# First attention scores issued between the last projection products, and the first keys loaded from ScalarE's queue

## The chip, the cores and the metric

One core of one Trainium2 chip runs the whole kernel. The metric is the device time of one execution in microseconds (us); a smaller one is better. The time before is 1726.04 us, the median of 3 runs (1724.21 to 1727.97).

## The reference, cut to what matters

A transformer block on `x` of 2048 rows by 512, with 32 heads of width 16, all in float32:

```python
mod = (silu(c) @ w_mod).reshape(1, 6, 1, -1)        # sa, ca, ga, sb, cb, gb
h = layernorm(x) * (1 + ca) + sa
q, k, v = heads(h @ wqkv)                            # 3 x (32, 2048, 16)
p = softmax(q @ k.T * 16 ** -0.5)                    # (32, 2048, 2048)
x = x + ga * ((p @ v) @ wo)
h = layernorm(x) * (1 + cb) + sb
x = x + gb * (gelu(h @ w1 + b1) @ w2 + b2)
```

## The kernel before, in words

Each float32 operand of a projection is split into a high and a low part, and a product is three matmuls per 128 rows of contraction. The order of all work is written out by hand (`manual_schedule`): what a loop emits first on an engine runs first there. DMAs go out on SyncE's queue (SP), a few early ones on ScalarE's. All DMAs, of both queues, take eight semaphores in turn, and an issue waits until the DMA that used its semaphore before has landed; the next instruction of that queue waits behind it.

**Projections (up to about 265 us).** A loop over four blocks of 512 rows makes the first keys and queries (`proj_qk`, evacuated at L446 to L461, stored to DRAM at L464) and some values (`proj_v`, L486, stored at L488). `split_w` (L183, L184) makes weight parts, `mod_store` (L232) a small product. In the last block the kernel opens the tiles `kts` and issues, in this order on SP, the queries of unit 0 (`load_qm(0)`, six DMAs, L515), half of its keys (`build_k`, six DMAs, L504) and the queries of unit 1.

Then a loop over `items` (L773, L776) makes the remaining values, keys and queries, twelve matmul pairs an item, the second half of an item six places behind the first. Between them `half_slot` runs the first pass over the scores, which finds row maxima: a matmul L573 into a `mx` bank, for one half of the keys a Relu copy on ScalarE (L579), for the other a combined maximum on VectorE (L582). `evacuate` copies a finished item on ScalarE (L446), GpSimd splits it (L450, L451), SP stores it (L464).

A unit `u` is a group of four heads and a block of 512 queries; there are 32 units, the first four of group 0. `load_q(u)` brings a unit's queries into `qst` (six DMAs, L515) and then its maxima (two DMAs, L535). Before, `load_q(0)` is issued at item `nv + 19` and `load_q(1)` at `nv + 21`, both within the items loop.

**Attention (from about 265 us).** At its start SP issues the constant rows of a new key tile, twelve loads of 256 KB (keys of groups 1 and 3, L504), two rows `ga_b` and `gb_b`, and the values of group 1. The loop runs over steps `s`, sixteen for each unit, in an order of tokens:

```python
ORDER = ("X0 X1 M1 X2 M0 X3 P M1".split(), "X0 X1 X2 M0 M0 X3 P M1".split())
ORDER_END = "X0 X1 X2 X3 P".split()       # step 0 and the last unit
```

X0 to X3 are `exp_step`: a matmul L1010 of 128 keys (stationary) with the unit's 512 queries and an Exp on ScalarE (L1011) into a tile `p`. M is one matmul and reduce of the remaining maxima (L554, L556). P is `pv_step` of the step before: eight matmuls L843. After a unit's last P, L830 copies its output. Step 16 is the first that reads `qst` of unit 1. `load_q(u + 1)` stands in step `16 u + 2` for `u` of 1 and more.

PSUM has eight banks. In the items loop three are the ring `sc` and five the ring `mx`; for attention they are dealt out again (four `sc`, three `mx`, one `pv`).

Of the kernel before, what the change touches and what calls it, by code (L numbers as in the profile page):

```python
# [16 lines left out]
P = 128  # L17
# [20 lines left out]
NU1 = len(FRONT) - 1  # L38
LAG = 6
REST_AT = 3  # L40
OP0 = 1
OPN = 4
NWARM = 18
# [10 lines left out]
def block_kernel(ctx: ExitStack, tc: tile.TileContext, x, wqkv, wo, w1, b1, w2, b2, c, w_mod, out):  # L54
# [439 lines left out]
    def heads(src, g, part, a, t0, t1):  # L494
        r0 = (g % 2) * 64
        ap = src[part, r0 : r0 + 64, t0:t1]
        return ap.rearrange("(p a d) t -> a d p t", a=2, d=DH)[a]

    def build_k(dst, src, g, t0=0, t1=S, parts=(0, 1, 2)):
        for i in parts:  # L500
            part = (0, 0, 1)[i]
            for a in range(2):
                r0 = a * 64 + i * DH
                sy.dma_start(dst[r0 : r0 + DH, :, t0:t1].bitcast(F32), heads(src, g, part, a, t0, t1))  # L504

    def load_k(g, tile):
        kst[g] = tile
# [29 lines left out]
    def one_rows(k):  # L537
        for a in range(2):
            r0 = a * 64 + KR
            sy.dma_start(k[r0 : r0 + 2].bitcast(F32), one_d[:, None, :].to_broadcast([2, 2, S]))  # L540

    mxs, left, vpos = {}, {}, {}

# [91 lines left out]
    for b in range(NB):  # L635
        if b == NB - 1:
            close(lcm)
            kcm, kpool = pool("kpool")
            kts = [kpool.tile([P, 2, S], FR, name=f"kt{i}") for i in range(2)]
            qmcm, qmpool = pool("qmpool")  # L640
            kd[0], kd[1] = kts
            load_qm(0)
            build_k(kts[0], kd_d[0], 0, 0, 2 * TB)
            load_qm(1)
        if b:
            if b + 1 < NB:
                xn = ln1(b + 1)()
            if b + 2 < NB:
                load_x(b + 2)
        accs = first  # L650
        if b:

            accs = {w: bank() for w in (1, 0)}
            terms = {w: terms3(*qk_args(b, 0, w)) for w in (1, 0)}
            n1 = 2 * KC
            for i0, i1 in ((0, n1), (n1, len(terms[0]))):
                for w in (1, 0):
                    for i in range(i0, i1):
                        te.matmul(accs[w], *terms[w][i], start=i == 0, stop=i == len(terms[w]) - 1)
        proj(proj_qk, b, 0, 1, accs[1])  # L660
        if b == 1:
            load_w(1)
            st[0] = sy
        if b == NB - 1:
            rest()
            rest = lambda: None
            split_w(1)
        proj(proj_qk, b, 0, 0, accs[0])
        if b == 0:
            xn = ln1(1)()  # L670
        if b == NB - 1:
            mod_store(mrow)
            break
        if b == 1:
            mod_cols(1, mrow)
        for _ in range(V_A[b][0]):
            proj(proj_v, *vitems.pop(0), len(vitems) == 15)
        ln1_t(b + 1, xn)
        for _ in range(V_A[b][1]):
            proj(proj_v, *vitems.pop(0))  # L680
        if b < 2:
            mrow = mod_rows(wms)
        if b == 0:
            wms = [load_wm(2, 0), load_wm(5, 1)]
# [36 lines left out]
    for n in range(N + 2):  # L721
        if n == 1:
            close(acm)
        if n == 0:
            build_k(kts[0], kd_d[0], 0, 2 * TB, S)
        if n == 3:
            load_qm(FRONT[2])
        if n == 5:
            load_w(2)
        if n == 7:  # L730
            build_k(kts[1], kd_d[0], 1)
        if n == nv + 5:
# [12 lines left out]
        if n == nv + 10:  # L745
            kd[2] = kts[0]
            build_k(kts[0], kd_d[1], 2)
        if n == nv + 16:
            load_v(0)
        if n == nv + 19:  # L750
            load_k(2, kts[0])
        if n == nv + 19:
            load_q(0)
        if n == nv + 21:
            load_q(1)
        if n < N:
            k, b, w = items[n]
            if k and b == 2 and w and k < 3:
                split_w(k + 1)
            if n:  # L760
                acc[n] = bank()
                terms[n] = terms3(*qk_args(b, k, w)) if k else terms3(*v_args(b, w), late_b=False)
        new = []
        if n == 0:
            rest()
            rest = evacuate(0)
        for i in range(NT if n else 0):


            m, j = divmod(n * NT + i - NT - LAG, NT)  # L770
            if n < N:
                p, q = terms[n][i]
                te.matmul(acc[n], p[:64], q[:64], start=i == 0, stop=False)  # L773
            if 0 < m < N:
                p, q = terms[m][j]
                te.matmul(acc[m], p[64:], q[64:], start=False, stop=j == NT - 1)  # L776
            t = n * NT + i - NT
            for _ in range(len(slots) * (t + 1) // NS_B - len(slots) * t // NS_B):
                visit()
            if i == REST_AT:  # L780
                rest()
                rest = lambda: None
            if 0 < m < N and j == NT - 1:
                rest = evacuate(m)
                if m == N - 1:
                    break
        for q in (late, todo):
            if q:
                q.pop(0)()
        todo += new  # L790
    rest()
    close(wcm)
    close(hcm)
    close(tcm)

    sc, mx = rings["sc"], rings["mx"]
    set_rings(sc=(sc[0], sc[1], mx[0], sc[2]), mx=mx[1:4], pv=mx[4:])


    pcm, ppool = pool("ppool", bufs=2)  # L800
# [1 line left out]
    one_rows(kq[1])  # L802
    load_k(1, kts[1])
    load_k(3, kq[1])
    epool = ctx.enter_context(tc.tile_pool(name="epool", bufs=1, side="right"))

    wo_hi = epool.tile([P, KC, D], FR, name="wo_hi")
    wo_lo = epool.tile([P, KC, D], FR, name="wo_lo")
    x2a = [epool.tile([P, 4, D], F32, name=f"x2a{i}") for i in range(2)]
    b2_b, ga_b, gb_b = [epool.tile([P, D], F32, name=n) for n in ("b2_b", "ga_b", "gb_b")]  # L810
    for i, t in enumerate((ga_b, gb_b)):
        sy.dma_start(t, bass.AP(tensor=g_d.tensor, offset=g_d[i].offset, ap=[[0, P], [1, D]]))
    o_b = epool.tile([P, 4, D], F32, name="o_b")
    xn_b = epool.tile([P, 4, D], F32, name="xn_b")

    wo_r = {}

    def wo_load(k):
        wo_r[k] = epool.tile([P, D], F32, tag="h32", name="wo_raw", bufs=3)
        sy.dma_start(wo_r[k], wo[k * P : (k + 1) * P, :])  # L820
        if k == 0:
            sy.dma_start(b1_c, b1.rearrange("(f p) -> p f", p=P))
            sy.dma_start(b2_b, bass.AP(tensor=b2.tensor, offset=b2.offset, ap=[[0, P], [1, D]]))

    pt = {}

    def attn_out(u, pv):
        g, qb = divmod(u, NB)
# [23 lines left out]
    def at(s, f):  # L852
        hooks.setdefault(s, []).append(f)

    for k in range(KC):
        s0 = 20 + 8 * k
        at(s0, lambda k=k: wo_load(k))
        at(s0 + 3, lambda k=k: gp.tensor_tensor(wo_r[k], wo_r[k], ga_b, op=ALU.mult))
        at(s0 + 4, lambda k=k: ve.tensor_copy(wo_hi[:, k], wo_r[k]))
        at(s0 + 6, lambda k=k: gp.tensor_tensor(wo_lo[:, k], wo_r[k], wo_hi[:, k].bitcast(F32), op=ALU.subtract))  # L860
# [138 lines left out]
    for i, n in zip(range(4, 9), (12, 13, 13, 14, 14)):  # L999
        at(base + n, lambda i=i: run("l", lambda: ln2(0), i))  # L1000

    def exp_step(s, j):

        u, kc = divmod(s, NKC)
        q, k = qst[u], kst[u // NB]
        p, a = divmod(j, 2)
        ps = bank()
        pb = pt[s, j] = ppool.tile([P, TB], F32, tag="p", name="p", bufs=10)
        r0 = a * 64
        te.matmul(ps, k[r0 : r0 + KX, p, kc * P : (kc + 1) * P], q[r0 : r0 + KX, p], start=True, stop=True)  # L1010
        ac.activation(pb, ps, AF.Exp, scale=SCALE)  # L1011

    for s in range(NS):
        u, kc = divmod(s, NKC)
        g, qb = divmod(u, NB)
        if kc == 2 and 0 < u < NU - 1:
            load_q(u + 1)
        new = []
        for tok in ORDER[s % 2] if 0 < s < NS - NKC else ORDER_END:
            if tok[0] == "X":  # L1020
                exp_step(s, int(tok[1]))
            elif tok[0] == "P":
                if s:
# [12 lines left out]
    pv_step(NS - 1)  # L1036
    for cm in (pcm, qcm, vgcm, kqcm, qmcm):
        close(cm)


# [134 lines left out]
```

## Time and profile before

| what | value |
|---|---|
| median of 3 runs | 1726.04 us (1724.21 to 1727.97) |
| the profiled execution's own time | 1728.43 us |
| its span, from first to last instruction | 1726.7 us |
| mean granted TensorE clock | 0.993 |
| TensorE (PE) busy | 1715.8 us |
| VectorE (DVE) busy | 1389.9 us |
| ScalarE (ACT) busy | 1352.9 us |
| DMA queue q1, share of 16 engines | 32.6% |

PE is the matmul unit, PEld its weight loads, SPq the issuing of DMAs on SyncE's queue. A busy PE isn't PE at its peak: matmul ends are modelled, so the number of instructions in a stretch says more than its busy time. `PEclk` is the granted TensorE clock as a share of full speed. In the timeline a row has start, duration, engine, line, tiles and count; in brackets stands the idle time of the engine before it and what ended it.

### The profile page before, as it was taken

To read this page: it belongs to the slowest core of one execution; us is meant where nothing else is said; L and a number is where in the kernel's file an instruction comes from. 1 tells how busy PE (TensorE), PEld (TensorE's weight loads), DVE (VectorE), ACT (ScalarE), POOL (GpSimd) and SP (SyncE) were. 2 spreads that over 40 slices of the span, in tenths; PEclk is the share of its full clock that TensorE was granted. 3 is DMA by queue.
4 is the path that set the end of the run, shared out by engine and by line. 5 is a ranking of instruction groups with operands and counts; after the bars stand their busy time and mean duration, and the time that the engine had idled before them with its cause. 6 is when DMAs were issued, how large, how long until landed. Compare 5 with 4: busy or idle time off the path is not lost.

```text
span 1726.7 us, 29970 instructions
## 1 busy us (share of the span) xinstructions
PE 1715.8 (99%) x10968; PEld 905.6 (52%) x10968; DVE 1389.9 (80%) x2559; ACT 1352.9 (78%) x2580; POOL 312.7 (18%) x341
## 2 busy tenths in 40 slices
PE   9999999999999999999999999999999999999998
PEld 7766664333443334333433343334433488888887
DVE  6699997998888888888888888888885296746453
ACT  3588888999999999999999999999999632222222
POOL 3205430110000000000000000000022154636562
PEclk9899998999999999999999999999999999999999
DMA  9854988314112201400500110111023064423331
GB/s 328 223 124 153 172 177 162 73 41 60 40 36 44 55 24 33 69 23 24 88 23 23 43 33 24 39 32 27 23 66 106 19 204 131 138 79 110 99 122 49
DMA packets 125223, 144.22 MB, mean 84 GB/s; under 512 B 39026, under 2 KB 74866, under 8 KB 123124
## 3 DMA queue, kind: packets, MB, share of 16 engines
q1 hardware_dynamic: 123828, 139.71, 32.6%
q10 hardware_dynamic: 1248, 2.59, 0.4%
q8 instruction: 86, 1.41, 0.4%
q14 instruction: 61, 0.50, 0.1%
HBM read 106.37 MB, written 35.87 MB: 82 GB/s over the span
## 4 chain that ended last, share of the span: by engine, by line
PE 95%; DVE 2%; ACT 1%; SPq 1%; DMA 1%; issue 1%; POOL 0%; ACTq 0%
PE pv L843 30%; PE mx L554 20%; PE sc L1010 14%; PE sc L308 9%; PE mx L1074 6%; PE mx L573 5%; PE sc L776 4%; PE pv L1074 2%; PE sc L950 2%; PE sc L773 2%; PE mx L950 1%; PE sc L261 0%; PE sc L359 0%; DMA wmod<-in_w_mod_dram 0%; DVE bst L239 0%
## 5 line engine op out<-in xcount | busy, mean ns | idle before, releaser
L1011 ACT ACTIVATE p<-sc 128x512 f32<-128x512 f32 x2048 | 1054.7, 613 | 43.1 <-PE sc L1010 16.8
L556 DVE TENSOR_REDUCE mxs<-mx 128x1 f32<-128x512 f32 x1472 | 928.1, 683 | 118.8 <-PE sc L1010 91.4
L843 PE MATMUL pv<-p,vg 128*32 128x512 f32 x4096 | 548.1, 607 | 0.0
L1010 PE MATMUL sc<-qst,kq 50*128 50x512 f32 x1024 | 286.8, 438 | 0.3 <-ACT raw L446 0.3
L1010 PE MATMUL sc<-qst,kt 50*128 50x512 f32 x1024 | 282.5, 432 | 0.0
L554 PE MATMUL mx<-kq,qmx 48*128 48x512 f32 x768 | 262.5, 428 | 0.5 <-DVE mxs L556 0.4
L554 PEld LDWEIGHTS mx<-kq,qmx 48*128 48x128 f32 x768 | 121.9, 184 | 230.4 <-DVE mxs L556 212.1
L554 PE MATMUL mx<-kt,qmx 48*128 48x512 f32 x704 | 241.1, 430 | 0.0
L554 PEld LDWEIGHTS mx<-kt,qmx 48*128 48x128 f32 x704 | 113.6, 186 | 211.0 <-DVE mxs L556 191.5
L1053 ACT ACTIVATE g<-sc,b_c 128x512 f32<-128x512 f32 x56 | 38.6, 690 | 223.0 <-PE sc L308 218.5
L595 POOL CAST m<-mn 128x16 fp32r<-128x16 f32 x32 | 6.3, 198 | 1040.8 <-DVE mn L589 1040.8
L582 DVE CUSTOM_DVE_ANT_0 cp<-mx,cp 128x512 f32<-128x512 f32 x288 | 182.1, 686 | 14.0 <-PE mx L573 11.2
L573 PE MATMUL mx<-kt,qmx 48*128 48x512 f32 x576 | 181.1, 428 | 2.9 <-DMA qmx<-qk 1.2
L579 ACT ACTIVATE cp<-mx 128x512 f32<-128x512 f32 x288 | 157.2, 603 | 26.2 <-PE mx L573 20.9
L843 PEld LDWEIGHTS pv<-p,vg 128*32 128x32 f32 x4096 | 81.1, 108 | 181.3 <-issue 169.7
L1010 PEld LDWEIGHTS sc<-qst,kq 50*128 50x128 f32 x1024 | 126.8, 186 | 30.3 <-ACT p L1011 21.3
L573 PEld LDWEIGHTS mx<-kt,qmx 48*128 48x128 f32 x576 | 102.5, 190 | 57.7 <-DVE mxf L582 34.3
L1057 DVE TENSOR_TENSOR glo<-g,ghi 128x512 fp32r<-128x512 f32 x56 | 57.6, 1029 | 92.1 <-ACT ghi L1056 92.1
L1010 PEld LDWEIGHTS sc<-qst,kt 50*128 50x128 f32 x1024 | 125.6, 185 | 9.4 <-ACT p L1011 2.4
L879 POOL TENSOR_TENSOR w1l<-w1r,w1h 128x512 fp32r<-128x512 f32 x56 | 76.5, 1366 | 146.7 <-DVE w1h L878 123.1
L881 POOL TENSOR_TENSOR w2l<-w2r,w2h 128x512 fp32r<-128x512 f32 x56 | 82.5, 1473 | 6.2 <-DVE w2h L880 5.8
L308 PE MATMUL sc<-kt,w1h 128*128 128x512 f32 x224 | 73.8, 391 | 0.0
(185 smaller groups left out, 1912.5 us busy)
## 6 DMA issues: line engine op xcount, KB each, us to landing
qk<-parts SPq DMA_DIRECT2D x30, 512.0 KB
w1r<-in_B_w_dram SPq DMA_DIRECT2D x56, 256.0 KB
w2r<-in_B_w_dram SPq DMA_DIRECT2D x56, 256.0 KB
qmx<-qk SPq DMA_DIRECT2D x192, 64.0 KB
qst<-qk SPq DMA_DIRECT2D x192, 64.0 KB
kq<-qk SPq DMA_DIRECT2D x24, 256.0 KB
kt<-qk SPq DMA_DIRECT2D x24, 256.0 KB
vg<-v SPq DMA_DIRECT2D x8, 664.0 KB
```

Source lines behind the costliest of these rows:

```text
L308: te.matmul(ps, p, q, start=i == 0, stop=i == len(terms) - 1)
L554: te.matmul(ps, qmx[u][rows, p, qc * P : (qc + 1) * P], kst[u // NB][rows, p, kr * TB : (kr + 1) * TB], start=True, stop=True)
L556: ve.tensor_reduce(mxs[u][:, p, a, qc, kr : kr + 1], ps, axis=AX.X, op=ALU.max, negate=True)
L573: te.matmul(ps, qmx[u][rows, p, qc * P : (qc + 1) * P], kd[u // NB][rows, p, t0 : t0 + TB], start=True, stop=True)
L579: ac.activation(vpos[n, a], ps, AF.Relu)
L582: ve.tensor_tensor_reduce(v, ps, v, -1.0, 3.0e38, ALU.add, ALU.min, mxs[u][:, p, a, qc, r : r + 1])
L843: te.matmul(cur_pv[0][32 * j : 32 * (j + 1)], vg[g][:, kc, j * VW : j * VW + 32], pt.pop((s, j)), start=kc == 0, stop=kc == NKC - 1)
L879: gp.tensor_tensor(alo, a, ahi.bitcast(F32), op=ALU.subtract)
L881: gp.tensor_tensor(blo, b, bhi.bitcast(F32), op=ALU.subtract)
L1010: te.matmul(ps, k[r0 : r0 + KX, p, kc * P : (kc + 1) * P], q[r0 : r0 + KX, p], start=True, stop=True)
L1011: ac.activation(pb, ps, AF.Exp, scale=SCALE)
L1074: te.matmul(acc[qb][t], p[:, sl], q, start=f == 0 and n == 0, stop=f == NF - 1 and n == 2)
```

## The change

Three edits, and what they need.

1. `build_k` gets a queue as an argument. The six DMAs of unit 0's first keys go out on ScalarE's queue, and in program order they stand ahead of `load_qm(0)`, whose six DMAs stay on SP. In the order of instructions ScalarE's six stand behind the copy L486 and ahead of the copy L453 that evacuates the last block's first product; the fourth, fifth and sixth wait for semaphores that the first, third and fifth query DMA of unit 0 used.
2. The four `exp_step`s of step 0 run inside the items loop, between the last matmuls of the last item (places 9, 11, 13 and 15 of the tail that `FIRST_X` counts). They use two `sc` banks (the third holds the last item) and write to four tiles that exist already or are opened for them. Step 0 of the attention loop skips its X tokens. The pool `epool`, whose space overlaps two of these tiles, is opened after step 1.
3. `load_q(1)` moves from item `nv + 21` to step 2 of attention. On SP it then stands behind the constant rows, the twelve key loads, four stores of maxima, `ga_b`, `gb_b` and the values of group 1.

```diff
+FIRST_X = (9, 11, 13, 15)
...
-    def build_k(dst, src, g, t0=0, t1=S, parts=(0, 1, 2)):
-        for i in parts:
+    def build_k(dst, src, g, t0=0, t1=S, eng=sy):
+        for i in range(3):
...
-                sy.dma_start(dst[r0 : r0 + DH, :, t0:t1].bitcast(F32), heads(src, g, part, a, t0, t1))
+                eng.dma_start(dst[r0 : r0 + DH, :, t0:t1].bitcast(F32), heads(src, g, part, a, t0, t1))
...
+            build_k(kts[0], kd_d[0], 0, 0, 2 * TB, ac)
             load_qm(0)
-            build_k(kts[0], kd_d[0], 0, 0, 2 * TB)
             load_qm(1)
...
-        if n == nv + 21:
-            load_q(1)
+        if n == N:
...
+            first_p.extend([px, pm, wraw[:, 0], wraw[:, 1]])
...
+                if n == N - 1:
+                    last_sc = rings["sc"].pop()
...
+            if n >= N and (n - N) * NT + i in FIRST_X:
+                exp_step(0, FIRST_X.index((n - N) * NT + i))
...
-    set_rings(sc=(sc[0], sc[1], mx[0], sc[2]), mx=mx[1:4], pv=mx[4:])
+    set_rings(sc=(sc[0], mx[0], sc[1], last_sc), mx=mx[1:4], pv=mx[4:])
...
+    at(1, open_epool)
...
-        if kc == 2 and 0 < u < NU - 1:
+        if kc == 2 and u < NU - 1:
             load_q(u + 1)
...
             if tok[0] == "X":
-                exp_step(s, int(tok[1]))
+                if s:
+                    exp_step(s, int(tok[1]))
```

More of the change, by code (lines that the diff above doesn't have):

```diff
@@ L540, in one_rows, with exp_step @@
             sy.dma_start(k[r0 : r0 + 2].bitcast(F32), one_d[:, None, :].to_broadcast([2, 2, S]))
+    pt, first_p = {}, []
+    def exp_step(s, j):
+        u, kc = divmod(s, NKC)
+        q, k = qst[u], kst[u // NB]
+        p, a = divmod(j, 2)
+        ps = bank()
+        pb = pt[s, j] = ppool.tile([P, TB], F32, tag="p", name="p", bufs=10) if s else first_p[j]
+        r0 = a * 64
+        te.matmul(ps, k[r0 : r0 + KX, p, kc * P : (kc + 1) * P], q[r0 : r0 + KX, p], start=True, stop=True)
+        ac.activation(pb, ps, AF.Exp, scale=SCALE)
     mxs, left, vpos = {}, {}, {}
@@ L753, in block_kernel @@
             load_q(0)
-        if n == nv + 21:
-            load_q(1)
+        if n == N:
+            wraw = tpool.tile([P, 2, KC, P], F32, tag="wraw", name="p_w", bufs=1).rearrange("p a k n -> p a (k n)")
+            pm = tpool.tile([P, TB], F32, tag="pm", name="p_m", bufs=1)
+            pxcm, pxpool = pool("pxpool")
+            px = pxpool.tile([P, TB], F32, name="px")
+            first_p.extend([px, pm, wraw[:, 0], wraw[:, 1]])
         if n < N:
@@ L793, in block_kernel @@
     close(hcm)
-    close(tcm)
     sc, mx = rings["sc"], rings["mx"]
-    set_rings(sc=(sc[0], sc[1], mx[0], sc[2]), mx=mx[1:4], pv=mx[4:])
+    set_rings(sc=(sc[0], mx[0], sc[1], last_sc), mx=mx[1:4], pv=mx[4:])
     pcm, ppool = pool("ppool", bufs=2)
@@ L804, in block_kernel, with open_epool @@
     load_k(3, kq[1])
[L805 to L814, printed above, removed]
+    epool = wo_hi = wo_lo = x2a = b2_b = ga_b = gb_b = o_b = xn_b = None
+    def open_epool():
+        nonlocal epool, wo_hi, wo_lo, x2a, b2_b, ga_b, gb_b, o_b, xn_b
+        close(tcm)
+        epool = ctx.enter_context(tc.tile_pool(name="epool", bufs=1, side="right"))
+        wo_hi = epool.tile([P, KC, D], FR, name="wo_hi")
+        wo_lo = epool.tile([P, KC, D], FR, name="wo_lo")
+        x2a = [epool.tile([P, 4, D], F32, name=f"x2a{i}") for i in range(2)]
+        b2_b, ga_b, gb_b = [epool.tile([P, D], F32, name=n) for n in ("b2_b", "ga_b", "gb_b")]
+        for i, t in enumerate((ga_b, gb_b)):
+            sy.dma_start(t, bass.AP(tensor=g_d.tensor, offset=g_d[i].offset, ap=[[0, P], [1, D]]))
+        o_b = epool.tile([P, 4, D], F32, name="o_b")
+        xn_b = epool.tile([P, 4, D], F32, name="xn_b")
     wo_r = {}
@@ L823, in wo_load @@
             sy.dma_start(b2_b, bass.AP(tensor=b2.tensor, offset=b2.offset, ap=[[0, P], [1, D]]))
-    pt = {}
     def attn_out(u, pv):
@@ L1000, in block_kernel @@
         at(base + n, lambda i=i: run("l", lambda: ln2(0), i))
[L1002 to L1011, printed above, removed]
     for s in range(NS):
@@ L1036, in block_kernel @@
     pv_step(NS - 1)
-    for cm in (pcm, qcm, vgcm, kqcm, qmcm):
+    for cm in (pcm, pxcm, qcm, vgcm, kqcm, qmcm):
         close(cm)
```

## The prediction

> **What bounds the kernel now.** I read the page first, for the engine shares and the chain.
>
> ```profile
> PE 1715.8 (99%) x10968; PEld 905.6 (52%) x10968; DVE 1389.9 (80%) x2559; ACT 1352.9 (78%) x2580; POOL 312.7 (18%) x341
> PE 95%; DVE 2%; ACT 1%; SPq 1%; DMA 1%; issue 1%; POOL 0%; ACTq 0%
> ```
>
> TensorE is the chain. A microsecond in which it waits, or runs slowly, is lost unless another engine would have held it anyway. So I looked next, in tables by stretch, for time in which its clock fell. It did so in two places, both beside the change (columns: length, PE, PEld, DVE, ACT, POOL busy with counts, PEclk, DMA share, GB/s).
>
> ```profile
> 60.59:64.00 3.41, 3.41 (x17) 2.73 (x15) 0.00 (x0) 0.57 (x1) 0.93 (x1) 1.00 0.84 178
> 64.00:67.41 3.41, 3.41 (x14) 1.91 (x13) 1.98 (x3) 2.06 (x5) 0.79 (x1) 1.00 1.03 130
> 67.41:70.83 3.42, 2.26 (x10) 1.34 (x9) 0.69 (x1) 1.47 (x4) 1.73 (x2) 1.00 0.93 141
> 70.83:84.48 13.65, 13.65 (x52) 11.25 (x51) 7.85 (x23) 8.18 (x15) 0.00 (x0) 0.50 0.89 229
> 84.48:98.13 13.65, 13.44 (x104) 9.16 (x103) 12.83 (x41) 11.97 (x23) 0.00 (x0) 1.00 0.40 109
> 265.38:268.80 3.42, 3.12 (x16) 1.33 (x15) 2.31 (x10) 3.42 (x8) 1.73 (x4) 1.00 0.78 290
> 268.80:279.04 10.24, 10.24 (x45) 3.88 (x37) 5.27 (x9) 5.85 (x12) 0.52 (x1) 0.50 0.92 152
> 279.04:289.28 10.24, 10.24 (x75) 3.97 (x73) 8.84 (x15) 9.57 (x19) 0.00 (x0) 1.00 1.02 117
> ```
>
> After a thin stretch of matmuls (10 in 3.42 us, 16 in 3.42 us) the clock is at half, for 13.65 us and for 10.24 us. (The 14 and 17 ahead of 67.41 fill the 128 rows of the array; the 16 have 48 to 50 rows or 32 columns, as the rows below show of their kinds.) PE's busy time doesn't show it; the counts do. The first low clock costs between 13.65 x (1 - 23/41) = 6.0 us (by DVE's count) and 13.65 x (1 - 15/23) = 4.7 us (by ACT's); I take 5.3. For the second I count the P matmuls alone:
>
> ```profile
> 268.80:279.04 10.24, 4.82 (x24) 0.40 (x16) 0.50 0.92 152
> 279.04:289.28 10.24, 5.33 (x40) 0.79 (x40) 1.00 1.02 117
> ```
>
> 24 instead of 40: 10.24 x (1 - 24/40) = 4.1 us, or 0.4 us for each microsecond of low clock there.
>
> **Part 1, the tail of the projections.** Timeline of ScalarE and TensorE:
>
> ```profile
> 264.00 0.60 ACT L579 ACTIVATE cp<-mx 128x512 f32<-128x512 f32 x1 [0.33 <-PE mx L573]
> 265.24 0.60 ACT L446 ACTIVATE raw<-sc 128x512 f32<-128x512 f32 x1 [0.65 <-PE sc L776]
> 265.74 4.02 ACT L1011 ACTIVATE p<-sc 128x512 f32<-128x512 f32 x8
> ```
>
> Eight Exps in 4.02 us are 0.5 us each. Today all eight stand behind the last copy L446, and TensorE waits for them bank by bank. The change puts four (2.0 us) in front of that copy, where ScalarE has 0.33 + 0.65 = 1.0 us of idle time. So the copy comes 1.0 us later, and step 1's Exps start 1.0 us earlier. TensorE then has step 0's P at hand at once, and the thin stretch is filled. I expect the clock not to fall here: 1.0 + 4.1 = 5.1 us gained, if nothing later waits.
>
> **Part 2, `load_q(1)` behind the key loads.** This is what I weigh most. SP's queue, and TensorE at step 16:
>
> ```profile
> 253.49 3.83 SPq L515 DMA_DIRECT2D qst<-qk  x6
> ...
> 269.80 0.64 SPq L540 DMA_DIRECT2D kq<-one  x2
> 270.49 2.91 SPq L504 DMA_DIRECT2D kt<-qk  x6
> 275.22 11.32 SPq L504 DMA_DIRECT2D kq<-qk  x6
> ...
> 300.42 0.58 SPq L691 DMA_DIRECT2D vg<-v  x1
> 301.50 3.50 SPq L515 DMA_DIRECT2D qmx<-qk  x6
> ...
> 309.14 2.71 SPq L515 DMA_DIRECT2D qst<-qk  x6
> 311.89 1.28 SPq L535 DMA_DIRECT2D qst<-m  x2
> ```
> ```profile
> SPq L602 <- DMA kq<-qk: 7.0, 4, 1.8
> ```
> ```profile
> 303.57 0.72 PE L1010 MATMUL sc<-qst,kq 50*128 50x512 f32 x3
> ...
> 304.70 1.06 PE L843 MATMUL pv<-p,vg 128*32 128x512 f32 x8
> ```
> ```profile
> 306.06 0.63 ACT L830 ACTIVATE osb<-pv 128x512 f32<-128x512 f32 x1
> ```
>
> The P at 304.70 is unit 0's last, that of step 15: the copy of its output follows at 306.06. It stands within step 16, so the scores at 303.57 are step 16's, the first that need `load_q(1)`. Today that load is issued at 253.49, 50 us ahead. In the changed order it stands behind the twelve loads of 256 KB, directly behind the values `vg` and ahead of the `qmx` that was issued at 301.50. The DMA engines are full in that time (share 1.02 at 117 GB/s, the row from 279.04: 3.1 MB take 26 us), and the issues in between wait for these loads to land (the wait row). No row lets the queue go faster, and the change leaves the order ahead of it as it is.
>
> So `load_q(1)` is issued at about 301.5. Its eight DMAs take 4.0 us to issue (309.14 to 313.17 for unit 2), up to 305.5. How long the last takes to land no row tells directly: not below nothing, and not above the 4.0 us of a query DMA in the chain on a full queue (below). I take 2.5, as that queue is emptier by then. The last copy's 1.0 us delay reaches the stores that start this queue in part (GpSimd waits there for VectorE as well): 0.5. Step 16 can start at 305.5 + 2.5 + 0.5 = 308.5, from 306 to 310. Part 1 moves the wish for it to 303.57 - 5.1 = 298.5. TensorE issues in order, so the M and P tokens behind stand too, for 10 us, and ScalarE and VectorE run dry. Against before, step 16 starts 308.5 - 303.57 = **4.9 us later**. All that part 1 wins is eaten here, whether its clock stays up or not: the load sets the time.
>
> **Part 3, the clock after that wait.** Ten idle microseconds are far more than the thin stretches that brought the clock down twice. The same steps follow as from 268.80, so a low microsecond costs 0.4. If the low clock is counted from early in the wait, as long as 10.24 us, 2 us of it fall on work: 0.8. If it lasts 13.65 us of work: 5.5. I take the middle, **3.0 us**.
>
> The Trainium skill, page "TensorE: Matmul & The Clock Gate", section "Part 1: The HAM clock gate", says that the full clock returns after about 3.4 us of sustained work. By that the cost would be 3.4 x 0.4 = 1.4 us, an estimate from the page. This trace disagrees: under steady work the clock stayed low for 10.24 and 13.65 us.
>
> **Part 4, first keys on ScalarE's queue.** The start of the first pass:
>
> ```profile
> 56.88 4.29 SPq L515 DMA_DIRECT2D qmx<-qk  x6
> 61.21 3.98 SPq L504 DMA_DIRECT2D kt<-kd  x6
> 65.23 3.77 SPq L515 DMA_DIRECT2D qmx<-qk  x6
> ```
> ```profile
> 66.09 3.99 DMA qmx<-qk
> ```
> ```profile
> 59.21 0.60 ACT L486 ACTIVATE vst<-sc 128x512 f32<-128x512 f32 x1
> 63.43 0.60 ACT L453 ACTIVATE parts<-sc 128x512 fp32r<-128x512 f32 x1 [3.62 <-PE sc L659]
> 64.23 0.09 PEld L232 LDWEIGHTS sc<-mrow,sel 128*2 128x2 f32 x2 [0.35 <-ACT parts L453]
> 70.06 0.47 PE L573 MATMUL mx<-kt,qmx 48*128 48x512 f32 x1 [1.16 <-DMA qmx<-qk]
> ```
>
> ScalarE is free for the keys from 59.8, 1.4 us before SP gets to them. But the DMA engines are at 0.84 from 60.59 to 64.00, so an earlier issue finds 0.16 x 3.41 = 0.5 us of free time, and the queries of unit 1, behind the keys today, now compete with them. At most the 1.16 us wait before L573 goes. The cost is on ScalarE. The sixth key DMA waits for unit 0's fifth query DMA (of the six from 56.88, so issued at 60 to 61), which lands 2.5 to 4.0 us later, or later still where keys share the engines with it. Behind it stand L453, which frees a bank for L232, and TensorE in order after that. ScalarE is free at 63.6 to 65.9, against L453's 63.43: 0.2 to 2.5 us, 1.5 taken. That idle time comes at 64.3 instead of 68.9. The two nearly cancel in time, but a thin stretch is left and may only be earlier. Taken: the low clock stays and the sum is 0.7 us worse (from 0.5 better to 2.5 worse).
>
> **Sum.** 0.7 + 4.9 + 3.0 = **8.6 us slower**. The profiled execution took 1728.4 us, 2.4 more than the median of the runs; on the median the forecast is 1726.0 + 8.6 = **1734.6 us**. Ends of this case: -0.5 + 2.5 + 0.8 = +2.8, and 2.5 + 6.5 + 5.5 = +14.5.
>
> **Rivals.**
>
> *The first low clock goes.* If ScalarE's delay is under about 1.2 us, the idle time is spread over two stretches, neither as thin as 10 matmuls in 3.42 us. Then part 4 is -5.3 + 0.1, and the sum -5.2 + 4.9 + 3.0 = +2.7 us: 1728.7 us, from -0.5 to +6. For it: the row from 64.00 has 14 matmuls and can lose a few. Against it: the delay's upper end. The page "DMA: Bandwidth & Descriptors" of the Trainium skill, section "Issuing engines are not separate DMA queues", also speaks against it: issuing from a second engine saves only the sequencer's time.
>
> *The load is there in time, and the kernel is faster.* If the keys went at 160 GB/s or more and unit 1's queries landed by 298.5, nothing would wait at step 16: 0.7 - 5.1 = -4.4 us, 1721.6 us, and about 1716 if the first low clock goes too. It decides at 298.5. Against it: 117 GB/s at a share of 1.02.
>
> *Step 0 moves but the second clock drop stays.* ScalarE is then still too late at 266. The wish for step 16 is at 302.6 instead of 298.5 and the wait 6 us: the same end, within the forecast's range.
>
> **How the numbers follow.** About 0.2% (3.5 us) is what a measurement of this kernel can tell from no change. Forecast 0.64, the first clock's rival 0.26, the faster rival 0.10. Nearly all of the forecast is above +3.5, and 0.4 of the second: slower 0.64 + 0.10 = 0.74; the rest of the second is the same, 0.16; faster 0.10. The range leaves the faster rival and the two outer ends: 1727.5 to 1738.5.
>
> **What would show it.** A wait of L1010 on `qst`'s load at about 298, some 10 us long, with `load_q(1)` issued after `vg`; a half clock after it; no half clock at 268.8; at 63 to 66 ScalarE's copy L453 late, and L232 behind it. The forecast is wrong if unit 1's queries land before step 16, or if step 16 waits under 3 us.

## The result and the profile after

The changed kernel takes 1737.04 us (median of 6 runs, 1734.70 to 1743.13), the kernel before 1724.73 us beside it (6 runs, 1719.27 to 1727.97). The ratio is 1.0076, 95% interval [1.0054, 1.0098]: slower by 12.3 us on the medians and 13.1 by the ratio. The forecast was 1734.6 us, 1727.5 to 1738.5. The profiled execution after took 1738.45 us with a span of 1736.7, 10.0 more than the span before. Its trace starts 0.3 us later than that of before, so times of day are compared with that in mind. One run of a later kernel, the one with 13 extra matmuls, took 2151.47 us at a mean granted clock of 0.705 and counts nowhere below.

The file is longer, so lines have moved: L1010, L1011 (scores, Exp) are now L554, L555; the old L554, L556 (M) are L569, L571; L573, L579 are L588, L594; L843 (P) is L869; L453 is L455, L232 is L234, L446 is L448; the loads L504, L515, L535 are L506, L517, L537.

The page after, shares of the engines and of the chain:

```profile
PE 1715.5 (99%) x10968; PEld 904.9 (52%) x10968; DVE 1390.0 (80%) x2559; ACT 1352.5 (78%) x2580; POOL 312.4 (18%) x341
PE 92%; DVE 3%; DMA 3%; ACT 1%; issue 1%; SPq 0%; POOL 0%; ACTq 0%; DVEq 0%; POOLq 0%
```

The work is the same, but the chain now holds 3% of DMA where it had 1%. TensorE at step 16 and SP's queue in the timeline after:

```profile
299.74 0.50 PE L569 MATMUL mx<-kt,qmx 48*128 48x512 f32 x1
301.60 0.57 SPq L706 DMA_DIRECT2D vg<-v  x1
302.58 3.75 SPq L517 DMA_DIRECT2D qst<-qk  x6
306.37 1.76 SPq L537 DMA_DIRECT2D qst<-m  x2
308.88 1.60 PE L554 MATMUL sc<-qst,kq 50*128 50x512 f32 x3 [8.64 <-DMA qst<-m]
309.67 0.60 ACT L555 ACTIVATE p<-sc 128x512 f32<-128x512 f32 x1 [9.41 <-PE sc L554]
```

TensorE stands 8.64 us for the two DMAs of unit 1's maxima, which are the last two of the moved load's eight. They are issued behind the values `vg`, and step 16 starts 0.75 us after SP is done with their issue (306.37 + 1.76 = 308.13). The clock, by stretch, after (columns as in the prediction's tables):

```profile
64.32:67.73 3.41, 3.41 (x14) 1.95 (x13) 0.31 (x1) 0.60 (x1) 0.00 (x0) 1.00 1.05 142
67.73:71.15 3.42, 1.46 (x6) 0.61 (x4) 1.90 (x4) 2.41 (x5) 1.18 (x1) 1.00 0.60 132
71.15:84.80 13.65, 13.13 (x46) 10.74 (x48) 6.76 (x19) 7.75 (x14) 1.31 (x2) 0.50 0.89 223
265.38:268.80 3.42, 3.23 (x19) 2.14 (x21) 3.12 (x11) 3.42 (x9) 0.00 (x0) 1.00 0.42 156
268.80:279.04 10.24, 10.14 (x72) 3.82 (x66) 8.84 (x15) 9.31 (x19) 2.25 (x4) 1.00 0.74 132
303.25:316.91 13.66, 7.99 (x29) 2.70 (x29) 3.27 (x5) 4.83 (x9) 0.00 (x0) 0.50 0.50 119
316.91:330.56 13.65, 13.65 (x101) 5.69 (x97) 11.87 (x20) 12.71 (x25) 1.70 (x3) 1.00 0.35 69
```

The low clock at 268.80 is gone: 72 matmuls in that stretch where there were 45. A new one starts within the wait and covers 8 us of the work behind it. The first, near 71, is as long as before.

To see where time is won and lost, the starts of the same Exps of attention in both traces are compared one by one (the Exp of that number, the first of attention being 0; 4 is step 1's first, 64 step 16's):

| Exp | before, us | after, us | after minus before |
|---|---|---|---|
| 4 | 267.65 | 267.66 | +0.01 |
| 20 | 280.83 | 277.00 | -3.83 |
| 60 | 302.02 | 298.19 | -3.83 |
| 64 | 304.13 | 309.67 | +5.54 |
| 68 | 306.54 | 313.95 | +7.41 |
| 80 | 312.80 | 321.76 | +8.96 |
| 2040 | 1369.99 | 1379.67 | +9.68 |

3.83 us ahead up to the wait, 8.96 behind after it: step 16 costs 12.8 us. This number, the swing at step 16, serves below. It doesn't depend on where a trace starts.

### The profile page after: what moved, and what is told of

It is laid out like the page before. It is cut to its first block, busy times and chain, and to the rows that moved or that the text cites. A ratio compares the mean times of both kernels' runs of the same rounds, so it can differ in the third digit from the quotient of the medians.

```text
span 1736.7 us, 29972 instructions
## 1 busy us (share of the span) xinstructions
PE 1715.5 (99%) x10968; PEld 904.9 (52%) x10968; DVE 1390.0 (80%) x2559; ACT 1352.5 (78%) x2580; POOL 312.4 (18%) x341
## 4 chain that ended last, share of the span: by engine, by line
PE 92%; DVE 3%; DMA 3%; ACT 1%; issue 1%; SPq 0%; POOL 0%; ACTq 0%; DVEq 0%; POOLq 0%
PE pv L869 29%; PE mx L569 19%; PE sc L554 13%; PE sc L310 9%; PE mx L1091 6%; PE mx L588 5%; PE sc L798 3%; PE pv L1091 2%; PE sc L977 2%; PE sc L795 1%; DMA kq<-qk 1%; DMA kt<-qk 1%; PE mx L977 1%; DVE cp L597 0%; PE sc L263 0%
## 5 line engine op out<-in xcount | busy, mean ns | idle before, releaser
L555 ACT ACTIVATE p<-sc 128x512 f32<-128x512 f32 x2044 | 1053.1, 615 | 51.2 <-PE sc L554 25.2
L571 DVE TENSOR_REDUCE mxs<-mx 128x1 f32<-128x512 f32 x1472 | 928.4, 684 | 126.3 <-PE sc L554 77.7
L869 PE MATMUL pv<-p,vg 128*32 128x512 f32 x4088 | 546.7, 606 | 0.0
L554 PE MATMUL sc<-qst,kq 50*128 50x512 f32 x1024 | 286.5, 437 | 8.8 <-DMA qst<-m 8.6
L554 PE MATMUL sc<-qst,kt 50*128 50x512 f32 x1024 | 282.5, 432 | 0.0
L569 PE MATMUL mx<-kq,qmx 48*128 48x512 f32 x768 | 262.5, 428 | 0.5 <-DVE mxs L571 0.4
L569 PEld LDWEIGHTS mx<-kq,qmx 48*128 48x128 f32 x768 | 122.0, 184 | 230.4 <-DVE mxs L571 212.1
L569 PE MATMUL mx<-kt,qmx 48*128 48x512 f32 x704 | 240.8, 429 | 0.1
L569 PEld LDWEIGHTS mx<-kt,qmx 48*128 48x128 f32 x704 | 113.2, 185 | 210.8 <-DVE mxs L571 192.2
L588 PE MATMUL mx<-kt,qmx 48*128 48x512 f32 x576 | 181.0, 427 | 4.2 <-DVE parts L456 2.5
L594 ACT ACTIVATE cp<-mx 128x512 f32<-128x512 f32 x288 | 157.3, 604 | 24.6 <-PE mx L588 19.1
L869 PEld LDWEIGHTS pv<-p,vg 128*32 128x32 f32 x4088 | 81.0, 108 | 181.1 <-issue 169.2
L554 PEld LDWEIGHTS sc<-qst,kq 50*128 50x128 f32 x1024 | 126.6, 186 | 38.8 <-ACT p L555 20.2
L588 PEld LDWEIGHTS mx<-kt,qmx 48*128 48x128 f32 x576 | 103.1, 190 | 58.6 <-DVE mxf L597 34.2
L554 PEld LDWEIGHTS sc<-qst,kt 50*128 50x128 f32 x1024 | 125.6, 185 | 9.7 <-ACT p L555 2.4
```

Source lines behind the costliest of these rows:

```text
L569: te.matmul(ps, qmx[u][rows, p, qc * P : (qc + 1) * P], kst[u // NB][rows, p, kr * TB : (kr + 1) * TB], start=True, stop=True)
L571: ve.tensor_reduce(mxs[u][:, p, a, qc, kr : kr + 1], ps, axis=AX.X, op=ALU.max, negate=True)
L588: te.matmul(ps, qmx[u][rows, p, qc * P : (qc + 1) * P], kd[u // NB][rows, p, t0 : t0 + TB], start=True, stop=True)
L594: ac.activation(vpos[n, a], ps, AF.Relu)
L869: te.matmul(cur_pv[0][32 * j : 32 * (j + 1)], vg[g][:, kc, j * VW : j * VW + 32], pt.pop((s, j)), start=kc == 0, stop=kc == NKC - 1)
```

## Experiments

### The place of the load

**The changed kernel with `load_q(1)` back in the items loop.**

```diff
+        if n == nv + 21:
+            load_q(1)
         if n == N:
...
-        if kc == 2 and u < NU - 1:
+        if kc == 2 and 0 < u < NU - 1:
```

> The changed kernel with load_q(1) back at item nv + 21; the keys on ScalarE's queue and the early step 0 stay. Theory (the load behind the twelve key loads is the whole loss): no wait at step 16 and no half clock behind it, so 8.6 us of wait and 3.2 us of low clock go; Exp number 64 stands 3 to 4 us ahead of before, as the changed kernel stood up to step 15: about 1721 us, 3.5 to 4.5 us under before. Rival (early scores or keys on ScalarE cost the time): it stays 8 us or more over before.

Measured: 1723.96 us (12 runs), ratio to before 1.0004 [0.9988, 1.0020]. The swing is 0.0 (4.77 us ahead at Exps 60, 64 and 80). Windows of this kernel:

```profile
70.08:83.74 13.66, 13.03 (x46) 10.72 (x48) 6.87 (x19) 7.87 (x14) 1.42 (x2) 0.50 0.88 227
303.25:316.91 13.66, 13.66 (x97) 5.65 (x95) 12.04 (x21) 13.31 (x27) 1.70 (x3) 1.00 0.63 140
```

Only the first low clock is left. The place of this one load is worth 1737.04 - 1723.96 = 13.1 us, or 11.9 when each of the two is taken against the runs of before beside it (12.3 - 0.4); the rival is out. But the rest of the change doesn't gain the 3.5 to 4.5 us that were expected of it: with the load back it takes 0.4 us more than before.

**The kernel before with only that load moved.**

```diff
-        if n == nv + 21:
-            load_q(1)
...
-        if kc == 2 and 0 < u < NU - 1:
+        if kc == 2 and u < NU - 1:
```

> Before with only load_q(1) moved to step 2. Theory (the load sets when step 16 starts, whatever comes ahead): step 16 starts near 308, 4 to 5 us after before's 303.57, a wait of 4 to 5 us, then a low clock of 2 to 4 us: 7 to 9 us over before. Rival (the wait adds the same 8.6 us wherever the kernel stands): 11 to 13 us over before. Second rival (a wait of 5 us is too short to bring the clock down again): 4 to 5 us over before.

Measured: 1732.85 us (8 runs), ratio 1.0054 [1.0030, 1.0077]. Its timeline (L1008 are the scores):

```profile
298.61 0.57 SPq L691 DMA_DIRECT2D vg<-v  x1
299.63 3.73 SPq L515 DMA_DIRECT2D qst<-qk  x6
305.92 1.42 PE L1008 MATMUL sc<-qst,kq 50*128 50x512 f32 x3 [5.51 <-DMA qst<-m]
```

The wait comes without the other edits too, and in this profile the clock is at half from 303.21 to 313.45 us, so the second rival is out. On the medians it is 9.3 us over before, a little above the 7 to 9 expected, and under the first rival's 11 to 13. But step 16 starts at 305.92, not near 308: with the other edits the queue is 3 us later (`vg` at 301.60 instead of 298.61, though Exp number 60 comes at 298.19 and 298.37). The reason is the last copy of the items loop (L446 before, L448 after). SP stores that item first and only then issues the constant rows, 4.5 us after the copy's start in every trace here:

| trace | last copy | constant rows | `vg` | step 16 |
|---|---|---|---|---|
| before (load early) | 265.24 | 269.80 | 300.42 | 303.57 |
| only the load moved | 263.15 | 267.71 | 298.61 | 305.92 |
| after | 267.18 | 271.69 | 301.60 | 308.88 |
| after, 50-row fill (below) | 264.83 | 269.31 | 298.99 | 306.27 |
| after, P-form fill (below) | 264.46 | 268.96 | 299.20 | 306.61 |

With the load late, step 16 comes 41.4 to 42.8 us behind that copy. So the load has no fixed time: what is won ahead of the last copy brings the load forward too, and only what is won behind the copy is lost in the wait. The other two edits put the copy itself later. Of the 4.0 us between the second and the third row, some is also the longer low clock near 71 us in that trace (13.65 against 10.24 us), and 0.8 the later start of the trace.

**The changed kernel with `load_q(1)` at the start of attention, ahead of the twelve key loads.**

```diff
+    load_q(1)
     load_k(1, kts[1])
     load_k(3, kq[1])
...
-        if kc == 2 and u < NU - 1:
+        if kc == 2 and 0 < u < NU - 1:
```

> The changed kernel with load_q(1) at the start of attention too, but ahead of the twelve key loads on SP instead of behind them. Theory (only the place on SP matters, not the stage): no wait at step 16, the same time as e1, about 1724. Rival (a load issued after the items loop comes too late in any place, as the constant rows and stores hold the queue): a wait of L1010's counterpart on qst at step 16 of 1 us or more, 1726 or more.

Measured: 1730.01 us (6 runs), ratio 1.0036 [1.0022, 1.0050]; about 6 us above what was expected. There is no wait at step 16 (4.84 us ahead at Exp 64), so the rival's reason is out, though its time (1726 or more) is met. The loss comes later:

```profile
317.89 0.39 SPq L849 DMA_DIRECT2D wo_raw<-in_A_wo_dram  x1
322.29 0.43 DVE L887 CAST wo_hi<-wo_raw 128x512 fp32r<-128x512 f32 x1 [2.47 <-POOL wo_raw L886]
323.37 0.49 PE L569 MATMUL mx<-kt,qmx 48*128 48x512 f32 x1 [1.93 <-DVE mxs L571]
```
```profile
323.95:334.19 10.24, 10.22 (x40) 3.20 (x40) 5.72 (x9) 5.32 (x10) 1.39 (x2) 0.50 0.24 60
```

The first part of the output weights, due on VectorE at 319.8, is now the late load: SP issues it at 317.89, GpSimd has to scale it first, VectorE stands 2.47 us with TensorE's maxima behind it, and the clock falls. In the first experiment SP issues it at 312.35, and VectorE doesn't wait. Moving one load forward in a queue that is backed up moved the wait to a later load.

### The other two edits, each alone

**The kernel before with only the keys on ScalarE's queue.**

```diff
-            load_qm(0)
-            build_k(kts[0], kd_d[0], 0, 0, 2 * TB)
+            build_k(kts[0], kd_d[0], 0, 0, 2 * TB, ac)
+            load_qm(0)
```

(`build_k` gets its queue as an argument, as in the change.)

> Before with only the first keys on ScalarE's queue. Theory: the sixth key DMA holds ScalarE until 66.8, L453 is 3 us late, the first matmul of the first pass starts 1.0 to 1.5 us later than before, the half clock of 13.65 us stays: 1 to 2 us over before. Rival (the low clock comes and goes with the idle time): without it 4 to 5 us under before.

Measured: 1727.09 us (12 runs), ratio 1.0023 [1.0006, 1.0039]: 3.5 us slower, dearer than either size expected. Windows of this kernel:

```profile
72.35:86.01 13.66, 13.66 (x54) 11.53 (x54) 8.40 (x24) 7.92 (x14) 0.00 (x0) 0.50 0.85 194
268.80:279.04 10.24, 10.24 (x74) 4.01 (x74) 8.84 (x14) 9.98 (x20) 1.41 (x2) 1.00 0.93 186
```

The first low clock is there. The second, at 268.80, is not, though step 0 stands where it stood before. So the second one can stay away without the early scores. Beside the profile of before this shows what it costs: from Exp 4 to Exp 20 the kernel before takes 280.83 - 267.65 = 13.2 us, this one 277.19 - 268.62 = 8.6. That is 4.6 us.

**The first experiment with the keys back on SP, so that only the early scores are left.**

```diff
-            build_k(kts[0], kd_d[0], 0, 0, 2 * TB, ac)
             load_qm(0)
+            build_k(kts[0], kd_d[0], 0, 0, 2 * TB)
```

> Before with only the early step 0 (load_q(1) at nv + 21, keys on SP). Theory: the Exps of step 1 start 1 us earlier, the half clock at 268.8 goes: 1.0 + 4.1 = 5.1 us under before, about 0.3%. Rival (the clock falls a little later anyway): 1 us under before.

Measured: 1721.01 us (12 runs), ratio 0.9988 [0.9971, 1.0005]: 2.5 us by the medians, with an interval that reaches no change; four runs lie at 1716.7 to 1716.8, eight at 1720.8 to 1724.0. Its windows:

```profile
70.96:81.20 10.24, 10.24 (x40) 8.35 (x39) 6.52 (x19) 5.86 (x11) 0.00 (x0) 0.50 0.87 181
268.80:279.04 10.24, 10.24 (x77) 3.89 (x73) 9.21 (x15) 9.89 (x20) 0.00 (x0) 1.00 1.07 158
```

So on the medians the early scores gain 2.5 us (against before) to 3.1 (the first experiment against the keys alone, 1727.09 - 1723.96), and the keys cost 2.9 (1723.96 - 1721.01) to 3.5. The two cancel. Where two traces have the same low clocks, the early scores gain less: Exp 20 comes at 277.19 with the keys alone and at 276.05 in the first experiment, 1.1 us earlier. The rest of the gain on the medians is low clock.

### The first low clock

Beside the experiments so far the kernel before ran 31 times, between 1717.0 and 1730.8 us. The mean granted clock of each run shows why they differ: the six runs at 1.000 took 1717.0 to 1718.1 us, the four at 0.993 or less 1727.9 to 1730.8, and the straight line through all 31 loses 0.45 us for each microsecond at half clock (correlation 0.99; the time at half clock is worked out as twice what the mean lacks of 1, times the span). So the low clocks come in part of the runs only, and an edit that takes one away gains less on the median than in the one trace. The early scores alone show the same: their four runs at 1716.7 to 1716.8 have a clock of 1.000, the other eight 0.996 to 0.997.

Three kernels take the first low clock away, with extra matmuls that fill the wait ahead of the first pass.

**Before, and the early scores alone, each with six such matmuls** (the second kernel has the same edit):

```diff
             t = n * NT + i - NT
+            if t == 0:
+                spare = bank_mx()
+                for f in range(6):
+                    te.matmul(spare, w_hi[4][:, f % KC, :P], hT[0][0][:, f % KC], start=True, stop=True)
```

> Before with six extra matmuls of 128 rows and 512 columns (1.3 us of work, results unused) in the idle time before the first matmul of the first pass. Theory (a thin stretch of about 3.4 us brings the clock down): the half clock at 71 does not come, 4 to 5 us under those runs of before that have it; as not all of them do, 2 to 5 us under before's median, and the runs lie closer together. Rival (the clock falls because of the half-array matmuls of the first pass, not the idle time): same as before.

> e4 (early step 0 alone) with the six extra matmuls of e7. Theory: neither half clock comes in any run: 1716 to 1718 us in all of them, the lower group of e4's times, 6 us under before. Rival (e4's lower group has another cause): the two groups stay.

Measured: before with them 1722.22 us (12 runs from 1718.15 to 1728.06), ratio 0.9994 [0.9983, 1.0006]. The early scores with them 1717.81 us (5 runs, all within 1717.23 to 1718.98), ratio 0.9968 [0.9955, 0.9980]: of all kernels here the only one with a clear gain over before. Windows of the latter:

```profile
67.41:70.83 3.42, 3.42 (x15) 2.36 (x16) 0.00 (x0) 1.33 (x3) 0.89 (x1) 1.00 0.89 227
70.83:84.48 13.65, 13.46 (x95) 9.47 (x94) 12.50 (x41) 12.10 (x23) 0.00 (x0) 1.00 0.90 213
```

15 matmuls instead of 10 in the thin stretch, and 41 of VectorE's instructions instead of before's 23 in the next. With the first low clock filled away and the early scores, every run has a mean clock of 0.999 or 1.000 and the spread goes. With the fill alone it stays, against what was expected: the median is 1.75 us under before with an interval that reaches no change, seven runs have a clock of 0.998 or more (1718.15 to 1722.33 us) and five 0.995 or less (1724.47 to 1728.06). Its one profile, of 1718.15 us, has the full clock in both places; where the five slower runs lost theirs is not on record. Against the profile of before, Exp 4 comes 6.0 us earlier in it, 0.8 of them the earlier start of the trace: the first low clock costs 5.2 us.

**The first experiment (keys on ScalarE's queue) with 13 such matmuls**, into a bank that is free there:

```diff
+            if t == 0:
+                spare = psum[rings["mx"][-1]].tile([P, TB], F32, tag="b", name="mx")
+                for f in range(13):
+                    te.matmul(spare, w_hi[4][:, f % KC, :P], hT[0][0][:, f % KC], start=True, stop=True)
```

> The changed kernel with load_q(1) back in the items loop (as the first experiment), and 13 extra full matmuls ahead of the first pass, into a bank that is free there; they fill the wait of about 2.3 us before the first first-pass matmul. Beside the experiment with the extra matmuls and early scores (1717.8 us) it differs in the place of the key loads alone (and in the number of extra matmuls). Theory: the keys on ScalarE's queue cost twice, a start of the first pass that is 1.3 us later, and a low clock that is always there. With the extra matmuls the second part goes: no half clock near 71 us, and a time of 1717.8 + 1.3 to 1.5, about 1719.2 us. Rival: the low clock is not what is behind it (the late start alone, or DMA traffic, costs all of 2.9 us): the time stays above 1720.5 us even where no half clock is seen. If the extra matmuls themselves run longer than the wait, each adds 0.2 us or so.

Measured: 1719.98 us (median of 11 runs, 1719.20 to 1721.06), ratio 0.9987 [0.9973, 1.0001]. In its profile, of 1719.91 us, the clock is full from 6.92 us to the last us. Its timeline:

```profile
68.09 3.31 PE L807 MATMUL mx<-hThi,wv 128*128 128x512 f32 x13
71.33 0.72 PE L588 MATMUL mx<-kt,qmx 48*128 48x512 f32 x2
```

The first pass starts at 71.33, where without the extra matmuls it starts at 70.71, so 0.6 us of them is too much. 1719.98 - 0.6 = 1719.4 is 1.6 us above the early scores alone with a full clock (1717.81), where 1.3 to 1.5 was expected. So of the 2.9 to 3.5 us that the keys cost, about half is the later first pass. The rest is low clock: all twelve runs of the first experiment have a mean clock of 0.995 to 0.997 and lie 2.7 us and more over that 1719.4, the eleven here have 0.999 or 1.000, and of the twelve with the keys on SP four have 1.000. That the keys make the low clock come in every run fits their longer wait ahead of the first pass (2.48 us after, 1.16 before).

### The price of the low clock after the wait

Three kernels fill the wait at step 16 of the changed kernel with extra matmuls, to keep the clock up while the load stays late.

**68 matmuls of the form of the scores (50 rows).**

```diff
         new = []
+        if s == NKC:
+            spare = [bank(), bank()]
+            for i in range(68):
+                r0 = i % 2 * 64
+                te.matmul(spare[i % 2], kst[0][r0 : r0 + KX, 0, :P], qst[0][r0 : r0 + KX, 0], start=True, stop=True)
```

> The changed kernel with 68 extra matmuls (50 rows, 512 columns, results unused) in front of step 16's first score, some 7.8 us of work in the wait for unit 1's queries. Theory (the clock falls because TensorE idles, and the fall costs 3.2 us on top of the wait): step 16 starts when it did (near 308.9), no half clock at 303 to 317: 3 us under the changed kernel, about 1734. Rival (the wait alone is the price, the steps behind it are held by the loads anyway): the same 1737.

Measured: 1734.75 us (6 runs), ratio 1.0067 [1.0053, 1.0080]. The fill took 8.38 us, and the clock fell all the same, at 308.36 (windows of this kernel):

```profile
304.94:308.36 3.42, 2.55 (x17) 1.24 (x17) 0.53 (x1) 1.36 (x3) 0.00 (x0) 1.00 0.38 90
308.36:315.19 6.83, 6.83 (x30) 2.52 (x22) 3.58 (x7) 4.45 (x9) 0.00 (x0) 0.50 0.26 69
```

The swing is 12.4 us (-6.19 to +6.19). The time is near the 1734 that was expected, but not for the reason given, since the half clock came. The price of the clock can't be told from this run alone.

**Matmuls of the form of P, four side by side over all 128 rows and columns: first 17 groups and one more between the first two scores, then 10 groups.**

```diff
+        def fill(k):
+            for j in range(4 * k):
+                te.matmul(spare[32 * (j % 4) : 32 * (j % 4) + 32], vg[0][:, 0, :32], first_p[0], start=True, stop=True)
+
+        if s == NKC:
+            spare = bank_mx()
+            fill(10)
```

> The changed kernel with 68 extra matmuls ahead of step 16 and 4 between its first two scores, of the form of the P matmuls (128 rows and 32 columns, four side by side fill the whole array, 0.13 us each in step 16), where the earlier fill used half-height ones of 50 rows and the clock still fell for 6.83 us after it. They fill the wait of 8.6 to 9.7 us for the queries and maxima of unit 1 and add at most about 0.7 us behind it. Theory: the low clock after the wait costs about 0.4 us per microsecond, so 2.7 to 3.2 us; without it the loss at step 16 falls from 12.8 to about 9.6 to 10.3 us, and the time from 1737.0 to about 1733.8 (1733 to 1735). Rival: the restart itself (four banks, ScalarE and VectorE run dry) costs that time, whatever the clock: no half clock near 308 and still a loss over 12 us at step 16, a time of 1736 or more. Third case: the half clock comes all the same, and what it costs stays open.

> As the run before, with fewer extra matmuls: ten groups of eight (a float32 matmul of this kind is two instructions; seventeen groups took 14.8 us, so ten take 8.7 us), none between the scores. They fit the wait, which ends at about 306.3 us. The run before had no half clock after the wait, and lost 1.0 us from the first to the tenth Exp of the restart, where the changed kernel and the half-height fill lost 3.4 to 3.6 us at half clock. Theory: that difference, 2.4 to 2.6 us, is the price of the low clock; so against the half-height fill (1734.75 us) the time is 2.5 us lower, about 1732.3 us (1731.5 to 1733.2), with the Exps 3.6 to 3.9 us late behind step 16 where the first is 2.6 us late. Rival: the restart of the run before was short only because its longer fill gave ScalarE and VectorE time to clear what lay before them; then the restart costs over 2 us here too at full clock, and the time is 1733.5 us or more. Third case: the half clock comes again; then the two can't be told apart here.

Measured: the 17 groups 1739.40 us (4 runs), ratio 1.0092 [1.0075, 1.0109]. Each of these matmuls is two instructions, so the fill ran 14.80 us, past the load, and the time says nothing of the price; but no half clock came behind it. The 10 groups 1733.89 us (7 runs, 1731.82 to 1734.66), ratio 1.0061 [1.0039, 1.0083]; the profiled execution took 1731.82. Timeline and windows of the latter:

```profile
297.43 8.79 PE L1036 MATMUL mx<-px,vg 128*32 128x512 f32 x80
306.61 0.99 PE L554 MATMUL sc<-qst,kq 50*128 50x512 f32 x3 [0.39 <-DMA qst<-m]
```
```profile
306.66:316.90 10.24, 10.21 (x71) 4.15 (x74) 8.00 (x13) 9.68 (x20) 0.00 (x0) 1.00 0.33 92
```

The load is as late as ever, but the clock stays full: 71 matmuls in 10.24 us behind the wait. The Exps go from 6.56 us ahead to 2.97 behind at number 64 and 3.08 at number 80. The swing is 9.64 us, nearly all of it wait, and the restart at full clock costs 0.1 (Exp 64 to 80). With the half-height fill, where step 16 is about as late (Exp 64 2.64 behind), the same 16 Exps lose 3.55 us at half clock, and in the changed kernel 8.96 - 5.54 = 3.42. So the low clock behind the wait costs 12.79 - 9.64 = 3.2 us in these traces. The restart as such is not what costs; that rival is out in the trace. The median doesn't show it: 1733.89 lies outside the 1731.5 to 1733.2 expected, in what was put down for the rival, and only 0.9 us under the half-height fill. The mean clocks say why: three of the seven runs have 0.995 against the profiled one's 0.997, some 7 us more at half clock. Where in the run that lies is not on record.

## Why the prediction was right, and where its sizes were off

**Part 2, the load: right.** Predicted were an issue at 301.5 and a start of step 16 at 308.5 (306 to 310). They came at 302.58 and 308.88: 1.1 us later in the queue, 0.7 us less behind it. That the load, not TensorE, sets the time of step 16 is shown by the first experiment: without the move the swing is zero. Two things in it don't hold. The delay of the last copy was taken to reach the queue by half, and it reached it in full: the copy starts 1.9 us later than before, and so do the constant rows. And "all that part 1 wins is eaten" is true only of what is won behind that copy. In the rival in which the load is there in time, 160 GB/s would not have been enough by the prediction's own numbers: 3.1 MB in 19 us instead of 26 bring 308.5 to between 301 and 302, not to 298.5.

**Part 3, the low clock: right,** 3.0 predicted, 3.2 measured. That the size is so close is partly luck: 3.0 was the middle of two cases, 2 us and 13.65 us of work at half clock, and neither came. It covered 8 us of work, at 0.4 us each, the rest of its 13.66 us lying in the wait. Its length is again not that of the Trainium skill, page "TensorE: Matmul & The Clock Gate", section "Part 1: The HAM clock gate". That section has the full clock back after about 3.4 us of sustained work, but here it stayed low for 8 us of it.

**Part 1, the tail: right in its mechanism, too large on the median.** Timeline of ScalarE after:

```profile
264.80 0.67 ACT L555 ACTIVATE p_m<-sc 128x512 f32<-128x512 f32 x1
265.75 0.70 ACT L555 ACTIVATE p_w<-sc 128x512 f32<-128x512 f32 x1
267.18 0.74 ACT L448 ACTIVATE raw<-sc 128x512 f32<-128x512 f32 x1
267.66 2.22 ACT L555 ACTIVATE p<-sc 128x512 f32<-128x512 f32 x4
```

Four Exps lie in front of the last copy, and no half clock follows at 268.8. Predicted were 5.1 us, less 0.7 from part 4; the profiled pair shows 3.83 ahead, 4.1 with the later start of the trace. Its two terms hold in traces that suit them: 1.0 was predicted for the earlier Exps, and 1.1 is measured between the keys alone and the first experiment; 4.1 for the low clock, and 4.6 is measured between before and the keys alone. On the medians the early scores are worth 2.5 to 3.1, because the low clock that they take away is not there in every run of before: runs with a mean clock of 1.000 have none, and the profile of the keys alone has none at 268.8. That the early scores do keep a low clock away is shown by the two kernels with six extra matmuls, which differ in them alone: with the early scores all five runs have a mean clock of 0.999 or more, without them three of twelve.

**Part 4, the keys: right in sign, its path wrong, its size too small on the median.** Timeline after:

```profile
59.73 7.01 ACTq L506 DMA_DIRECT2D kt<-kd  x5
64.52 1.02 PE L234 MATMUL sc<-mrow,sel 128*2 128x512 f32 x2
66.79 0.60 ACT L455 ACTIVATE parts<-sc 128x512 fp32r<-128x512 f32 x1 [6.71 <-DMA kt<-kd]
67.42 0.69 DVE L456 TENSOR_TENSOR parts<-sc,parts 128x512 fp32r<-128x512 f32 x1 [6.77 <-ACT parts L455]
71.67 1.08 PE L588 MATMUL mx<-kt,qmx 48*128 48x512 f32 x2 [2.48 <-DVE parts L456]
```

ScalarE was held to 66.79, 3.1 us later than before after the 0.3 us of offset, where 0.2 to 2.5 was predicted. L234 was not behind it, against the prediction: it runs at 64.52, in time. What waited was the first pass, for VectorE's L456, which reads the same product as ScalarE's copy L455. In the kernel the ring `mx` takes over banks that held those products, so the first pass can't start until both have read them; it starts 1.3 us later. The failing step is "frees a bank for L232": the bank's next user was taken from the order of the rows, not followed through the banks. Predicted were 0.7 us (from -0.5 to 2.5). In two traces with the same first low clock, before and the keys alone, Exp 4 comes at 267.65 and 268.62, 1.0 us later, or 1.5 with the starts of the traces: within the range. On the medians it is 2.9 to 3.5, beyond it, since with the keys on ScalarE a low clock is there in every run. That the keys gain nothing from another queue agrees with the page "DMA: Bandwidth & Descriptors" of the Trainium skill, section "Issuing engines are not separate DMA queues". In the runs they also cost, since the engine that issues them does other work.

**The sum.** On the profiled pair 8.6 us were predicted and the span grew by 10.0; on the medians 8.6 were predicted and 12.3 measured. The load is not where the difference lies: its wait of 10 us and its low clock of 3.0 make 13.0, and the swing at step 16 is 12.8. Parts 1 and 4 were put at -5.1 + 0.7 = -4.4 us, and the first experiment, which holds these two alone, takes 0.4 us more than before. Their low clocks were priced from the one profiled execution of before, which has both and lay 2.4 us above the median, and were then taken off that median as if every run had them. The low clock behind the wait is different: all six runs of the changed kernel have a mean clock of 0.994 or less, more than 20 us at half clock. 1728.43 + 8.6 = 1737.0 would have met the median; so close a hit would be luck, as the profiled execution after took 1738.45. Open: the 0.7 us that the Exps lose between number 80 and the last.

## What to carry to other kernels

A load is as late as what stands ahead of it in its queue: before moving one, find when the queue gets to it and who reads it first. Moving it part of the way can hand the wait to the next load. An engine that issues DMAs which wait for semaphores holds up its own work. Before pricing a drop of the clock from one trace, compare the mean clock and the time of every run, or fill the thin stretches first: with both low clocks gone, the five runs of a kernel agreed to 1.8 us here.

## What the runs showed of the hardware that was not expected

- The half clock came after stretches with little idle time: a wait of 1.16 us in 3.42 before the change, and 0.51 + 0.36 us in the half-height fill. Filling with 50-row matmuls didn't keep the clock up, filling with ones that use all rows did, for the same 8.4 to 8.8 us. This fits a clock that counts the rows at work, but the two fills also differ in their columns, in how many matmuls run side by side, and in the idle time behind them (0.87 against 0.39 us), and that was not taken apart.
- A low clock lasted 6.83 (half-height fill), 10.24 (early scores alone) or 13.65 us (before), in each of these with TensorE busy throughout. Within each trace all changes of the clock lie whole steps of 3.41 us apart: before, those at 84.48, 268.80 and 279.04 us come 4, 58 and 61 steps behind the one at 70.83. The work lies differently on these steps in each trace. That could be why a thin stretch brings the clock down in one run and not in another, but no run tests it.
- The five last DMAs of the keys held ScalarE for 7.01 us; before, SP issued all six in 3.98 us.
